# Two expert layers after a recurrent attention: the second one's weight conversion and loop order are changed

## The chip, the core and the metric

The kernel runs on one core of a Trainium2 chip. A core has a matrix engine (TensorE, PE in the rows, with PEld for its weight loads), a vector engine (VectorE, DVE), a scalar engine (ScalarE, ACT), a general engine (GpSimd, POOL) and SyncE (SP), which here issues all DMAs. Each engine works through its own queue in the order of the program and waits on semaphores of the others. SBUF is the on-chip memory of 128 partitions, PSUM the eight accumulator banks that PE writes. The metric is the device time of one execution in microseconds; lower is better.

## What is computed

A recurrent attention over 768 steps for 4 x 8 heads of width 40 gives a matrix x of 3072 tokens by 320. Two expert layers follow ("MoE 1" and "MoE 2"); no token is routed, all go through all weights:

```python
def _moe_ref(x, w_in, w_out):          # d_ff = 2048
    h = x @ w_in
    g = h * np.clip(h + 3.0, 0.0, 6.0) / 6.0
    return (g @ w_out).astype(np.float32)

def _moe2_ref(x, w_a, w_b, w_out):     # d_ff = 1536
    return ((x @ w_a) * (x @ w_b) @ w_out).astype(np.float32)
```

The expert weights come in as 64-bit floats. [...] Each float is then split into a rounded high part and a remainder, and a product is made of three matmuls (high x high, high x remainder, remainder x high).

## The kernel before

**Attention and MoE 1, side by side.** The attention is worked in chunks of 64 steps. `window(j)`, j = 0 to 11, lists the steps of chunk j (`op_a` to `op_g`, `prep_w`, `prep_kb`, ...). The table `MOE` sets behind which of them a step of MoE 1 stands (`up(i)` or `down(i)` of 256 tokens), and the word WEIGHT marks the places where a piece of weights is converted: seven in a window from j = 2 on. The list is the program's order on every engine. In window j, `t_store(j)` (L523) copies and sends off the triangular inverse that GpSimd has made (its ACT copy is L528); `op_a(j+1)`, `t_load(j+1)` and `t_start(j+1)` begin the next one: four stores to DRAM and a load that turn the layout (TA), then 62 GpSimd instructions in a row (L515, L518, the "solve"). Behind that, GpSimd has `prep_a(j+2)` (L453). `op_e` ends with two DVE instructions that write the mask product GH (L615), which `op_f`'s matmuls (L636) read. An `up` of MoE 1 is 16 matmuls of 256 columns, then on ACT a clipping (L313), on DVE the product (L314), on ACT the rounding (L129) and on DVE the remainder gl (L130); `down` is 12 matmuls of 320 columns and needs both parts.

**Conversion before.** `f32_steps` (L71) is one ACT instruction (L77) and five on DVE: L78 and L83 with one input, L80, L84 and L86 with two. `widen()` converts MoE 2's weights beside the attention: 68 pieces of 128 x 192. Each piece is loaded by SP, converted, and stored by SP as 32-bit floats to DRAM (`w2af`, `w2bf`, `w2of`). A window's seven WEIGHT places take seven pieces.

**MoE 1 after the attention.** Some 20 MoE 1 steps are left behind window 11. Between them stand `conv.go()` calls: they load the 32-bit floats and split them (ACT rounds, GpSimd and DVE by turns subtract), 16 of 36 pieces; the other 20 follow in the first group of MoE 2.

**MoE 2 before.** All weights lie split in SBUF. Outside runs g over six groups of 512 tokens, inside m over twelve blocks of 128 inner units. `up(g, m)` is 16 matmuls of 512 columns (two sums of eight, a and b), an ACT copy of a (L846), a DVE product (L848), and the split of it (L129, L130). `down(g, m-1)` follows, 12 matmuls of 320 columns into four accumulators, one for each 128 tokens; they collect all twelve m and are then copied out and stored (`store`). At m = 8 the next group's x is turned by PE (`trans`, L816 to L820).

Of the kernel before, what the change touches and what calls it, by code (L numbers as in the profile page):

```python
# [94 lines left out]
def attention_and_moe(ctx, tc, t, flag):  # L95
# [22 lines left out]
    w1 = m1.enter_context(tc.tile_pool(name="w1", bufs=1))  # L118
# [621 lines left out]
    WC = (("w2a", 3 * FF2), ("w2b", 3 * FF2), ("w2o", 12 * DM))  # L740
    w2f = {n: (dram.tile([128, c], F32, name=n + "f") if wide else t[n].rearrange("q k c -> q (k c)")) for n, c in WC}

    def widen():
        pieces = [(t[n].rearrange("q k c -> q (k c)")[:, c0:c0 + 192], w2f[n][:, c0:c0 + 192])
                  for n, cols in WC for c0 in range(0, cols if wide else 0, 192)]
        loaded, made = [], None
        for i in range(len(pieces) + 3):
            if made:
                sp.dma_start(out=made[0], in_=made[1])
                made = None  # L750
            if i < len(pieces):
                loaded.append((pieces[i][1], words(pieces[i][0], sp)))
            yield
            if loaded and (i > 1 or i >= len(pieces)):
                dst, st = loaded.pop(0)
                made = dst, from_words(st)
            yield

    def moe2_weights(pool):
        r = {}  # L760
        r["ah"] = pool.tile([128, 2, FF2], F32R, name="ah")
        r["al"] = pool.tile([128, 2, FF2], F32R, name="al")
        r["at"] = pool.tile([128, FF2], F32R, name="at")
        r["bh"] = pool.tile([128, 2, FF2], F32R, name="bh")
        r["bl"] = pool.tile([128, 2, FF2], F32R, name="bl")
        r["bt"] = pool.tile([128, FF2], F32R, name="bt")
        r["oh"] = pool.tile([128, 12, DM], F32R, name="oh")
        r["ol"] = pool.tile([128, 12, DM], F32R, name="ol")

        turn = [0]  # L770

        def load(src, n, sink, c0):
            st = wk1.tile([128, 384], F32, tag="ws", name="st", bufs=3)[:, 0:n]
            sp.dma_start(out=st, in_=src)

            def steps():
                turn[0] += 1
                yield sink(st, gp if turn[0] % 2 else ve)
            return n, steps()

        def up(nm, kt, cols):
            if kt < 2:
                return lambda st, eng: split(r[nm + "h"][:, kt, cols], r[nm + "l"][:, kt, cols], st, eng)
            return lambda st, eng: split_tail(r[nm + "t"][:, cols], st, eng)

        def dn(m):
            return lambda st, eng: split(r["oh"][:, m], r["ol"][:, m], st, eng)

        items = []
        for c in range(4):  # L790
            for kt in range(3):
                for nm in "ab":
                    c0 = kt * FF2 + 384 * c
                    items.append(((0, c), w2f["w2" + nm][:, c0:c0 + 384], 384, up(nm, kt, slice(384 * c, 384 * c + 384)), 0))
            items += [((1, m), w2f["w2o"][:, m * DM:m * DM + DM], DM, dn(m), 0) for m in range(3 * c, 3 * c + 3)]
        return r, Converter(items, load)

    def moe2(r, wk, xpool, conv):

        xs = {}  # L800

        def load_x(g):
            xin = xpool.tile([128, 4, 384], F32, tag="xin", name="xin")
            src = x2d[g * 512:(g + 1) * 512, :].rearrange("(n p) c -> p n c", p=128)
# [49 lines left out]
        def down(g, *ms):  # L854
# [14 lines left out]
            for m in ms:  # L869
                gs.pop((g, m))  # L870
# [348 lines left out]
```

## Time and profile before

| | us |
|---|---|
| median of 3 runs | 1393.04 (1391.51 to 1396.16) |
| profiled execution | 1393.52, span 1391.7 |
| busy: PE, DVE, POOL, ACT | 1144.8, 837.0, 526.3, 520.8 |
| start to 253 | windows 0 and 1, weights of MoE 1 converted |
| 253 to 933 | windows 2 to 11 |
| 933 to 977 | rest of MoE 1 |
| 977 to the end | MoE 2 |

Busy times are sums over stages with different limits; what binds in a stage has to be read from that stage. The profile dates each instruction, names what ended an engine's idle time in front of it ("<-"), and gives the granted clock of PE as a share of full speed (1.00 is 2.4 GHz, 0.50 is 1.2 GHz). A matmul's length in a row includes its way through the array; successive ones overlap, so a rate is read from start to start.

### The profile page before, as it was taken

To read this page: it belongs to the slowest core of one execution; us is meant where nothing else is said; L and a number is where in the kernel's file an instruction comes from. 1 tells how busy PE (TensorE), PEld (TensorE's weight loads), DVE (VectorE), ACT (ScalarE), POOL (GpSimd) and SP (SyncE) were. 2 spreads that over 40 slices of the span, in tenths; PEclk is the share of its full clock that TensorE was granted. 3 is DMA by queue.
4 is the path that set the end of the run, shared out by engine and by line. 5 is a ranking of instruction groups with operands and counts; after the bars stand their busy time and mean duration, and the time that the engine had idled before them with its cause. 6 is when DMAs were issued, how large, how long until landed. Compare 5 with 4: busy or idle time off the path is not lost.

```text
span 1391.7 us, 34838 instructions
## 1 busy us (share of the span) xinstructions
PE 1144.8 (82%) x14826; PEld 1039.0 (75%) x14826; DVE 837.0 (60%) x1297; ACT 520.8 (37%) x1071; POOL 526.3 (38%) x835
## 2 busy tenths in 40 slices
PE   1214439889798888888888889899999999999997
PEld 1214438878787787778878889799888888888886
DVE  7899777486867776777767776556532222222322
ACT  1243344445443444444344444345422222222221
POOL 4889008382818382747465656302200000000000
PEclk9998559989989899988898989899999999999999
DMA  6262451515142524242333333323410000000000
GB/s 175 50 161 68 108 137 30 138 53 141 58 115 68 130 72 119 74 125 76 106 96 107 95 92 80 97 74 105 128 28 20 24 19 23 20 23 20 2 18 22
DMA packets 139908, 107.82 MB, mean 77 GB/s; under 512 B 88448, under 2 KB 129024, under 8 KB 137728
## 3 DMA queue, kind: packets, MB, share of 16 engines
q1 hardware_dynamic: 139744, 105.51, 28.0%
q8 instruction: 118, 1.93, 0.6%
q14 instruction: 46, 0.38, 0.1%
HBM read 78.87 MB, written 26.61 MB: 76 GB/s over the span
## 4 chain that ended last, share of the span: by engine, by line
PE 39%; DVE 29%; DMA 11%; ACT 10%; issue 8%; SPq 2%; POOL 0%; DVEq 0%; ACTq 0%; POOLq 0%
PE att L842 19%; PE up L308 4%; PE ac L866 3%; PE ac L865 3%; PE ac L864 3%; DVE up L314 3%; DVE rw L448 3%; DVE cv L80 2%; DVE ws L84 2%; DMA n<-TA 2%; ACT sq L458 2%; ACT gh L129 2%; DVE ws L83 2%; DVE W L446 2%; ACT TA L528 2%
## 5 line engine op out<-in xcount | busy, mean ns | idle before, releaser
L515 POOL TENSOR_TENSOR TT<-TA,TN 64x31 f32<-64x31 f32 (+15 forms) x372 | 207.6, 558 | 323.9 <-DMA TA<-scr 295.5
L518 POOL TENSOR_TENSOR TN<-TN,TT 64x31 f32<-64x31 f32 (+15 forms) x372 | 220.1, 592 | 29.1
L848 DVE TENSOR_TENSOR g<-att,asb 128x512 f32<-128x512 f32 x72 | 49.8, 692 | 227.4 <-PE att L842 227.4
L328 PE MATMUL dn<-wo_h,gh 128*128 128x320 f32 x384 | 142.8, 372 | 14.7 <-ACT gh L129 14.6
L330 PE MATMUL dn<-wo_h,gl 128*128 128x320 f32 x384 | 135.1, 352 | 1.6 <-DVE gl L130 1.5
L329 PE MATMUL dn<-wo_l,gh 128*128 128x320 f32 x384 | 134.0, 349 | 0.0
L129 ACT CAST gh<-up 128x512 fp32r<-128x512 f32 x96 | 56.3, 586 | 185.4 <-DVE up L314 185.4
L308 PE MATMUL up<-xh,wi_h 128*128 128x256 f32 x384 | 108.2, 302 | 3.1 <-ACT xh L287 3.1
L130 DVE TENSOR_TENSOR gl<-up,gh 128x512 fp32r<-128x512 f32 x96 | 66.3, 691 | 62.6 <-ACT gh L129 62.6
L308 PE MATMUL up<-xh,wi_l 128*128 128x256 f32 x384 | 102.3, 288 | 0.0
L328 PEld LDWEIGHTS dn<-wo_h,gh 128*128 128x128 f32 x384 | 85.4, 222 | 20.6 <-ACT gh L129 16.1
L313 ACT ACTIVATE g<-up,bias 128x512 f32<-128x512 f32 x96 | 65.8, 686 | 91.8 <-PE up L308 90.7
L636 PE MATMUL att<-GH,KBT 128*64 128x64 f32 (+1 forms) x768 | 47.9, 285 | 62.0 <-DVE GH L615 60.7
L129 ACT CAST g2h<-g 128x512 fp32r<-128x512 f32 x72 | 44.7, 621 | 144.1 <-DVE g L848 144.1
L846 ACT COPY asb<-att 128x512 f32<-128x512 f32 x72 | 42.3, 587 | 147.6 <-PE att L842 147.6
L314 DVE SCALAR_TENSOR_TENSOR up<-g,up 128x512 f32<-128x512 f32 x96 | 66.0, 688 | 46.0 <-ACT g L313 46.0
L636 PEld LDWEIGHTS att<-GH,KBT 128*64 128x64 f32 (+1 forms) x768 | 39.7, 176 | 68.4 <-DVE GH L615 68.2
L864 PE MATMUL ac<-oh,g2h 128*128 128x320 f32 x288 | 88.8, 308 | 1.1 <-ACT g2h L129 1.1
L330 PEld LDWEIGHTS dn<-wo_h,gl 128*128 128x128 f32 x384 | 86.1, 224 | 4.6 <-DVE gl L130 4.6
L866 PE MATMUL ac<-oh,g2l 128*128 128x320 f32 x288 | 88.7, 308 | 0.2 <-DVE g2l L130 0.2
L865 PE MATMUL ac<-ol,g2h 128*128 128x320 f32 x288 | 88.8, 308 | 0.0
L448 DVE RECIPROCAL rw<-W 128x256 f32<-128x256 f32 x48 | 84.1, 1753 | 3.9 <-ACT sq L458 1.2
(170 smaller groups left out, 3050.8 us busy)
## 6 DMA issues: line engine op xcount, KB each, us to landing
RV<-in_rve_dram SPq DMA_DIRECT2D x24, 320.0 KB
KB<-in_kbe_dram SPq DMA_DIRECT2D x22, 320.0 KB
st<-in_w1i_dram SPq DMA_DIRECT2D x13, 384.0 KB
ws<-in_w2a_dram SPq DMA_DIRECT2D x24, 192.0 KB
ws<-in_w2b_dram SPq DMA_DIRECT2D x24, 192.0 KB
raw<-in_we_dram SPq DMA_DIRECT2D x24, 162.5 KB
LB<-in_ae_dram SPq DMA_DIRECT2D x24, 160.0 KB
VX<-in_vte_dram SPq DMA_DIRECT2D x24, 160.0 KB
```

The source lines that it names most:

```text
L129: ac.copy(out=hi, in_=src)
L308: mm(u[:, e], a_, b_, start=(n == 0), stop=(n == len(seq) - 1))
L328: mm(acc, gh[:, e, c0:c0 + 128], wo_h[:, m], start=(m == 0), stop=False)
L329: mm(acc, gh[:, e, c0:c0 + 128], wo_l[:, m], start=False, stop=False)
L330: mm(acc, gl[:, e, c0:c0 + 128], wo_h[:, m], start=False, stop=(m == 15))
L448: ve.reciprocal(out=rw, in_=w[:, :, 1:65])
L515: eng.tensor_tensor(out=tv, in0=TA[:, 0:u, u:u + 1].to_broadcast([nr, u, n]), in1=TN[:, u:u + 1, u:32].to_broadcast([nr, u, n]), op=ALU.mult)
L518: eng.tensor_tensor(out=TN[:, 0:u, u:32], in0=TN[:, 0:u, u:32], in1=tv, op=ALU.subtract)
L842: mm(u, a_, b_, start=(n == 0), stop=(n == len(seq) - 1))
L864: mm(acc, gh[:, sl], r["oh"][:, m], start=(m == 0), stop=False)
L865: mm(acc, gh[:, sl], r["ol"][:, m], start=False, stop=False)
L866: mm(acc, gl[:, sl], r["oh"][:, m], start=False, stop=(m == 11))
```

## The change

`widen()` and its 68 pieces are gone, and the windows' WEIGHT places stay empty once MoE 1's weights are converted. MoE 2 is turned round. Outside runs b over four blocks of three m (384 inner units), inside g over the six groups, then the three m. The four accumulators collect three m only; `total` then copies them to a sum on chip (b = 0; two by DVE, two by ACT) or adds them to it (b = 1 to 3; four DVE adds), 24 times four, and stores the sum after b = 3. All of x stays split in SBUF for the four passes. It is loaded and turned by 256 tokens (`trans(h)`), during the end of MoE 1 and the groups of block 0, one step behind another.

The weights come as words straight from the input: for each m two pieces of 256 columns for the rows 0 to 255 of a and b, one of 256 for the rest of both, and two of 160 columns for the output weights; 15 pieces a block, 60 in all. Each is loaded (two load buffers), converted by the same five DVE instructions and split, always with DVE. Block 0's 15 pieces stand in the end of MoE 1, a later block's in the steps of the block ahead of it, one a step. The product of a and b overwrites b's PSUM bank, which is then held until the remainder is made.

```diff
+        def ahead(self):
+            while self.todo and len(self.loaded) < 2:
...
+                    sp.dma_start(out=st[:, o:o + w].rearrange("q (k c) -> q k c", k=x.shape[1]), in_=x.bitcast(I32))
...
+        def go(self, last):
+
+            self.ahead()
+            if not self.loaded or self.loaded[0][0] > last:
+                return
+            m, i, st = self.loaded.pop(0)
+            if wide:
+                st = st.rearrange("q (c w) -> q c w", w=2)
+                cv = wk1.tile([128, 2, 256], I32, tag="cv", name="cv2", bufs=2)[:, :, 0:st.shape[1]]
+                w = to_f32(nc, st, cv[:, 0], cv[:, 1], st[:, :, 1])
...
+            if i < 2:
+                split(self.up[m][:, 4 * i:4 * i + 2], self.up[m][:, 4 * i + 2:4 * i + 4],
+                      w.rearrange("q (k c) -> q k c", k=2))
...
+            self.ahead()
...
-            ve.tensor_tensor(out=g_, in0=res[1], in1=asb, op=ALU.mult)
...
+            ve.tensor_tensor(out=res[1], in0=res[1], in1=asb, op=ALU.mult)
...
+        def total(g, b):
+            if b == 0:
+                sums[g] = (xr if g < 4 else left()).tile([128, 4, DM], F32, name=f"sum{g}")
+            for tt in range(4):
+                acc, o = accs[g][tt][:, 0:DM], sums[g][:, tt]
+                if b:
+                    ve.tensor_tensor(out=o, in0=acc, in1=o, op=ALU.add)
+                elif tt % 2:
+                    ac.copy(out=o, in_=acc)
+                else:
+                    ve.tensor_copy(out=o, in_=acc)
+                if (b + 1) * BLOCK == NM:
+                    r0 = 512 * g + 128 * tt
+                    sp.dma_start(out=t["out"][r0:r0 + 128, :], in_=o)
...
+            for b in range(NM // BLOCK):
+                for g in range(NG):
+                    for i in range(BLOCK):
+                        m = BLOCK * b + i
...
+                        up(g, m)
+                        if b == 0 and g + 1 < NG and i:
+                            trans(2 * g + 1 + i)
+                        if prev:
+                            down(*prev)
+                        prev = (g, m)
+                        if g or i:
+                            w2.go(BLOCK * b + 2 * BLOCK - 1)
...
         for j in range(NCH):
             for f in window(j):
...
-                    elif j:
-                        next(wide2, None)
-                        next(wide2, None)
...
             if n > WEIGHTS_2:
-                conv.go()
+                w2.go(BLOCK - 1)
             if n == RANGE:
                 decide()
+                load_x(0)
+        trans(0)
+        load_x(1)
         m1i.close()
-        wk2.append(c2.enter_context(tc.tile_pool(name="wk2", bufs=2, reuse_waits="tile")))
         mq.pop(0)()
-        trans_0()
+        trans(1)
         mq.pop(0)()
+        m1w.close()
```

Where instructions stand: DVE's queue in a window, from a store of Y to the second mask product GH. Before (cv and ws are buffers of one conversion each):

```order
L78 TENSOR_SCALAR ws<-cv_8146 128x192
L80 SCALAR_TENSOR_TENSOR cv_8146<-cv_8146,ws 128x192
L83 TENSOR_SCALAR ws<-cv_8146 128x192
L84 SCALAR_TENSOR_TENSOR ws<-ws 128x192
L86 TENSOR_TENSOR cv_8146<-cv_8146,ws 128x192
L615 TENSOR_TENSOR GH<-att,mask 128x512 x2
L78 TENSOR_SCALAR ws<-cv_8192 128x192
L80 SCALAR_TENSOR_TENSOR cv_8192<-cv_8192,ws 128x192
L83 TENSOR_SCALAR ws<-cv_8192 128x192
L84 SCALAR_TENSOR_TENSOR ws<-ws 128x192
L86 TENSOR_TENSOR cv_8192<-cv_8192,ws 128x192
L314 SCALAR_TENSOR_TENSOR up<-g,up 128x512
```

The same place in the changed kernel, DVE (its line numbers are one higher here):

```order
L638 TENSOR_TENSOR Y<-att,W_102 104x512
L616 TENSOR_TENSOR GH<-att,mask 128x512 x2
L315 SCALAR_TENSOR_TENSOR up<-g,up 128x512
L131 TENSOR_TENSOR gl<-up,gh 128x512
L638 TENSOR_TENSOR Y<-att,W_102 104x512
```

The ten conversion instructions around GH are gone; the rest stands as it stood.

DVE in the end of MoE 1, from xl (the remainder of the last 256 tokens) on. Before (bl is the remainder of a weight piece of b, x an output tile of MoE 1):

```order
L288 TENSOR_TENSOR xl<-xt,xh 128x768
L130 TENSOR_TENSOR bl<-st,bh 128x384
L334 TENSOR_SCALAR x_12158<-dn 128x320
L334 TENSOR_SCALAR x_12161<-dn 128x320
L314 SCALAR_TENSOR_TENSOR up<-g,up 128x512
L130 TENSOR_TENSOR gl<-up,gh 128x512
```

DVE at the same place in the changed kernel, from the third conversion to the fourth (up_11439 and dn_11528 are weight tiles of MoE 2, up without a number the PSUM bank of MoE 1):

```order
L78 TENSOR_SCALAR ws_11442<-cv_11486 128x256
L80 SCALAR_TENSOR_TENSOR cv_11486<-cv_11486,ws_11442 128x256
L83 TENSOR_SCALAR ws_11442<-cv_11486 128x256
L84 SCALAR_TENSOR_TENSOR ws_11442<-ws_11442 128x256
L86 TENSOR_TENSOR cv_11486<-cv_11486,ws_11442 128x256
L135 TENSOR_TENSOR up_11439<-cv_11486,up_11439 64x256
L315 SCALAR_TENSOR_TENSOR up<-g,up 128x512
L131 TENSOR_TENSOR gl<-up,gh 128x512
L78 TENSOR_SCALAR ws_11466<-cv_11521 128x160
L80 SCALAR_TENSOR_TENSOR cv_11521<-cv_11521,ws_11466 128x160
```

Where one subtraction stood between two products of MoE 1, there are now one or two whole conversions of six DVE instructions.

DVE in the first group of MoE 2 before (g and g2l are a product and its remainder, ol and al remainders of weights):

```order
L848 TENSOR_TENSOR g_12720<-att,asb 128x512
L130 TENSOR_TENSOR g2l<-g_12720,g2h 128x512
L130 TENSOR_TENSOR al<-st,ah 128x384
L848 TENSOR_TENSOR g_12770<-att,asb 128x512
L130 TENSOR_TENSOR g2l<-g_12770,g2h 128x512
```

DVE in one step of block 0 of the changed kernel (x2l is the remainder of the next group's x):

```order
L852 TENSOR_TENSOR att<-att,asb 128x512
L131 TENSOR_TENSOR g2l<-att,g2h 128x512
L832 TENSOR_TENSOR x2l_12409<-att,x2h_12408 128x3x128 x2
L78 TENSOR_SCALAR ws_12377<-cv_12498 128x256
L80 SCALAR_TENSOR_TENSOR cv_12498<-cv_12498,ws_12377 128x256
L83 TENSOR_SCALAR ws_12377<-cv_12498 128x256
L84 SCALAR_TENSOR_TENSOR ws_12377<-ws_12377 128x256
L86 TENSOR_TENSOR cv_12498<-cv_12498,ws_12377 128x256
L135 TENSOR_TENSOR up_12374<-cv_12498,up_12374 64x256
```

A whole conversion and the next group's x now stand behind the product of every step of block 0.

## Rows read from the trace of the kernel before

**Rows 1.** Stretches: length, busy us (xinstructions) PE PEld DVE ACT POOL; clock, DMA share, GB/s.

```profile
542.83:614.57 71.74, 60.34 (x1059) 56.00 (x1059) 52.65 (x80) 31.62 (x69) 40.84 (x66) 0.88 0.38 104
...
828.08:888.27 60.19, 55.38 (x1052) 52.52 (x1044) 39.01 (x68) 28.62 (x59) 33.59 (x62) 0.94 0.35 89
...
933.00:977.00 44.00, 43.08 (x324) 42.05 (x323) 26.05 (x39) 22.82 (x44) 9.31 (x9) 1.00 0.38 117
977.00:1391.70 414.70, 405.20 (x2083) 350.15 (x2081) 124.09 (x191) 107.38 (x196) 9.95 (x9) 0.99 0.09 28
```

**Rows 2.** Chain of waits, 200 to 960: start us, length us, link (two L528).

```profile
253.17 1.95 ACT TA L528
...
828.08 1.96 ACT TA L528
```

**Rows 3.** DVE by line, 200 to 900: xcount | busy us, mean ns | idle before.

```profile
L80 DVE SCALAR_TENSOR_TENSOR cv<-cv,ws 128x192 int32<-128x192 int32 x66 | 46.1, 698 | 2.3
L84 DVE SCALAR_TENSOR_TENSOR ws<-ws 128x192 f32<-128x192 uint32 (+1 forms) x67 | 42.7, 638 | 2.3
L86 DVE TENSOR_TENSOR cv<-cv,ws 128x192 f32<-128x192 f32 (+1 forms) x67 | 38.5, 575 | 2.3
...
L83 DVE TENSOR_SCALAR ws<-cv 128x192 int32<-128x192 int32 x66 | 30.4, 461 | 2.3
...
L78 DVE TENSOR_SCALAR ws<-cv 128x192 int32<-128x192 int32 x66 | 25.9, 392 | 5.3 <-ACT cv L77 5.3
```

**Rows 4.** Waits, 200 to 900: who for whom, total us, times, longest us.

```profile
PE att L636 <- DVE GH L615: 48.3, 27, 4.7
...
ACT cv L77 <- DMA w2bf<-cv: 25.8, 8, 6.5
```

**Rows 5.** PE in order of time, window 10: start us, length us, line [idle before].

```profile
875.49 2.53 PE L636 MATMUL att<-GH,KBT 128*64 128x64 f32 x32 [4.68 <-DVE GH L615]
...
879.18 0.47 PE L329 MATMUL dn<-wo_l,gh 128*128 128x320 f32 x1
```

**Rows 6.** GpSimd (POOL) in order of time, windows 6 and 10.

```profile
562.34 0.25 POOL L515 TENSOR_TENSOR TT<-TA,TN 64x31 f32<-64x31 f32 x1 [29.09 <-DMA TA<-scr]
...
602.06 4.96 POOL L453 TENSOR_TENSOR LB<-LB,W 64x1024 f32<-64x1024 f32 x2
...
845.45 0.25 POOL L515 TENSOR_TENSOR TT<-TA,TN 64x31 f32<-64x31 f32 x1 [23.21 <-DMA TA<-scr]
...
883.57 0.25 POOL L518 TENSOR_TENSOR TN<-TN,TT 64x31 f32<-64x31 f32 x1
```

**Rows 7.** DVE in order of time, one conversion while GpSimd is idle.

```profile
903.70 0.25 DVE L78 TENSOR_SCALAR ws<-cv 128x192 int32<-128x192 int32 x1
...
905.07 0.36 DVE L86 TENSOR_TENSOR cv<-cv,ws 128x192 f32<-128x192 f32 x1
```

**Rows 8.** DVE in order of time, MoE 1 after the attention.

```profile
944.50 0.96 DVE L288 TENSOR_TENSOR xl<-xt,xh 128x768 fp32r<-128x768 f32 x1
...
973.95 0.70 DVE L314 SCALAR_TENSOR_TENSOR up<-g,up 128x512 f32<-128x512 f32 x1 [0.46 <-ACT g L313]
975.30 0.69 DVE L130 TENSOR_TENSOR gl<-up,gh 128x512 fp32r<-128x512 f32 x1 [0.65 <-ACT gh L129]
```

**Rows 9.** DVE in order of time, two steps of MoE 2.

```profile
996.63 0.69 DVE L848 TENSOR_TENSOR g<-att,asb 128x512 f32<-128x512 f32 x1 [1.75 <-PE att L842]
998.01 0.69 DVE L130 TENSOR_TENSOR g2l<-g,g2h 128x512 fp32r<-128x512 f32 x1 [0.69 <-ACT g2h L129]
...
1002.13 0.69 DVE L848 TENSOR_TENSOR g<-att,asb 128x512 f32<-128x512 f32 x1 [2.28 <-PE att L842]
```

**Rows 10.** DVE and then ScalarE in order of time: the two halves of a split.

```profile
983.89 0.48 DVE L130 TENSOR_TENSOR ol<-st,oh 128x320 fp32r<-128x320 f32 x1
...
983.16 0.46 ACT L129 CAST oh<-st 128x320 fp32r<-128x320 f32 x1
```

**Rows 11.** PE in order of time, the last step of MoE 2.

```profile
1380.53 0.41 PE L864 MATMUL ac<-oh,g2h 128*128 128x320 f32 x1 [1.06 <-ACT g2h L129]
```

More of the change, by code (lines that the diff above doesn't have):

```diff
@@ L736, in window @@
         return out
[L740 to L796, printed above, removed]
@@ L805, in load_x, with moe2, trans @@
+    def moe2(w2, xr, left):
+        xins, xs, gs, accs = {}, {}, {}, {}
+        sums = {}
+        def load_x(h):
+            xin = wk1.tile([128, 2, 384], F32, tag=("xt", "xh", "xl")[(h - 1) % 3 if h > 1 else 0], name="xin", bufs=1)
+            src = x2d[h * 256:(h + 1) * 256, :].rearrange("(n p) c -> p n c", p=128)
             sp.dma_start(out=xin[:, :, 0:DM], in_=src)
             sp.dma_start(out=xin[:, :, DM:384], in_=src[:, :, 256:DM])
-            xs[g] = xin
-        def trans(g):
-            xin = xs.pop(g)
-            xh = wk().tile([128, 3, 512], F32R, tag="x2h", name="x2h")
-            xl = wk().tile([128, 3, 512], F32R, tag="x2l", name="x2l")
-            for n in range(4):
+            xins[h] = xin
+        def trans(h):
+            xin = xins.pop(h)
+            g, c = h // 2, 256 * (h % 2)
+            if h % 2 == 0:
+                pool = xr if g < 2 else left()
+                xs[g] = [pool.tile([128, 3, 512], F32R, name=f"x2{n}{g}") for n in "hl"]
+            xh, xl = xs[g]
+            for n in range(2):
@@ L817, in trans @@
                 pv = ps[:, 0:384].rearrange("q (k c) -> q k c", k=3)
-                ac.copy(out=xh[:, :, 128 * n:128 * n + 128], in_=pv)
-                ve.tensor_tensor(out=xl[:, :, 128 * n:128 * n + 128], in0=pv,
-                                 in1=xh[:, :, 128 * n:128 * n + 128].bitcast(F32), op=ALU.subtract)
-            xs[g] = (xh, xl)
-        NG = NT // 512
-        accs = {}
-        gs = {}
+                cols = slice(c + 128 * n, c + 128 * n + 128)
+                ac.copy(out=xh[:, :, cols], in_=pv)
+                ve.tensor_tensor(out=xl[:, :, cols], in0=pv, in1=xh[:, :, cols].bitcast(F32), op=ALU.subtract)
         def up(g, m):
-            conv.need(0, m // 3)
+            w2.need(m, False)
             xh, xl = xs[g]
-            f0 = 128 * m
+            w = w2.up[m]
             res = []
-            for nm in "ab":
+            for i in range(2):
                 u = bank()
@@ L881, in rest @@
         def rest():
-            load_x(1)
             prev = None
-            for g in range(NG):
-                for m in range(12):
-                    up(g, m)
-                    if g == 0:
-                        conv.go(3)
-                    if prev and (g, m) != (NG - 1, 11):
-                        down(*prev)
-                        prev = None
-                    prev = prev + (m,) if prev else (g, m)
-                    if m == 8 and g + 1 < NG:
-                        trans(g + 1)
-                        if g + 2 < NG:
-                            load_x(g + 2)
+            load_x(2)
@@ new lines, in rest @@
+            for b in range(NM // BLOCK):
+                for g in range(NG):
+                    for i in range(BLOCK):
+                        m = BLOCK * b + i
+                        if b == 0 and g + 1 < NG:
+                            h = 2 * g + 2 + i
+                            if i < 2:
+                                load_x(h + 1) if h + 1 < 2 * NG else None
+                        up(g, m)
[6 more added lines that the diff above has]
+                            w2.go(BLOCK * b + 2 * BLOCK - 1)
```

116 lines of the change are left out of this document (68 added, 48 removed).

## Prediction

> **What bounds the kernel now.** I read the stretches first, cut where window j of the attention begins its store (L528, t_store) [rows 1]. Two regimes show. From 977 us to the end (MoE 2) PE is busy 405.2 of 414.7 us at clock 0.99, while DVE works 124 us of it: PE bounds that stage, DVE is 70% idle. In the windows nothing is full: in window 6 PE is busy 60.3 of 71.7 us at granted clock 0.88, DVE 52.7, POOL 40.8. The chain of waits gives the length: L528 of window 2 at 253.17, of window 10 at 828.08 [rows 2], so eight windows of 71.9 us each. At full clock PE's work in a window is about 60.3 x 0.88 = 53 us (in window 10: 55.4 x 0.94 = 52 us). So some 19 us of a window are PE idle or at the lower clock.
>
> Then what holds PE there. The groups by line show the five DVE instructions of a conversion (L78 to L86): together 183.6 us of DVE between 200 and 900, 2.76 us for each of some 67 pieces, 19.3 us for the seven pieces of a window [rows 3]. They stand in DVE's queue between the MoE's products and the masks GH, and PE waits for GH 48.3 us in all; ACT stands besides, 25.8 us in one of several such rows, because a conversion buffer has not yet been written out [rows 4]. What such a wait costs shows in window 10: PE idles 4.68 us before L636, which then takes 2.53 us, and the matmuls of 320 columns after it have 0.47 us each [rows 5]; those are the rates of the lower clock level (1.2 of 2.4 GHz), granted after the idle time.
>
> Is there another limit just below 71.9? POOL's triangular solve is the candidate. In window 6 its data lands at 562.34, 19.5 us after L528, and it ends at 602.06, 39.7 us later; the next L528 comes at 614.57, 12.5 us after that. In window 10 it starts 17.4 us after L528 and takes 38.4 us [rows 1, 6].
>
> **Part 1, the windows.** The 68 pieces leave windows 2 to 11, with their ACT instruction and both DMAs; nothing else there is reordered (the first two fences of the change show DVE's queue at GH). DVE keeps 52.7 - 19.3 = 33.4 us of work per window. The floor from PE is 53 us. The floor from POOL is 19.5 + 39.7 = 59.2 us at window 6's prices, 17.4 + 38.4 = 55.8 us at window 10's, since L528 copies what the solve has made. Window 10 is a trial of the whole: it lacks the preparation of later windows, so DVE has 39.0 us there with the pieces still in, and it takes 60.2 us [rows 1]. The other windows would have a lighter DVE than that. I take 59.2, the POOL chain at the prices of the window itself, and keep 55.8 to 64.2 as bounds (64.2 is a rival below). Gain: 8 x (71.9 - 59.2) = 101.3 us. Window 10 falls from 60.2 to its POOL chain of 55.8: 4.4 us. Window 11 has no solve beside it and PE nearly full: nothing. Together 105.7 us. The matching SP work goes too, but SP only releases loads there; I cost it at nothing, covered by the POOL chain, which contains SP's transfers and is kept at today's 19.5.
>
> **Part 2, the end of MoE 1.** The first 15 pieces now stand between the last eight ups of MoE 1, two to most ups (the fourth fence). POOL does nothing beside them. A piece of 192 columns with POOL idle takes 1.73 us from 903.70 to 905.43 [rows 7]: 0.25 us with one input, 0.36 with two. With 0.48 us for 320 columns [rows 10] a column costs 0.94 ns, so 256 columns take 2 x 0.31 + 3 x 0.42 + gaps 0.15 = 2.03 us and 160 take 1.58. Then ACT rounds (0.46 at 320 columns [rows 10], so 0.40 and 0.31) with DVE waiting, and DVE subtracts (0.42 and 0.33); three hand-overs of 0.05. A piece holds DVE 3.0 us (nine of 256) or 2.4 us (six of 160): 41.4 us for 15. Each up needs 0.70 + 0.65 wait + 0.69 = 2.04 us of DVE [rows 8], and 0.3 more because ACT's clipping now stands behind a rounding: 2.34 x 8 = 18.7 us. With 0.9 us for two stores that is 61.0 us from the end of xl (945.46). Today the same stretch ends with gl at 975.99, 30.5 us after xl [rows 8]: PE sets the pace there, and the splits beside it hide. So DVE becomes the bound and the stage grows by 30.5 us; 1 us more for PE's lower clock when it starts again: **+31.5**. Bounds: +20 if the rounding hides behind the next piece, +46 if a piece costs what it costs beside POOL (2.76 x 256/192 = 3.7, with the split 4.5).
>
> **Part 3, MoE 2 itself.** The matmuls are the same, 16 of 512 and 12 of 320 columns a step, and a step is 5.50 us on PE (996.63 to 1002.13) [rows 9]. DVE has 2.07 us in it (product, wait for ACT, remainder [rows 9]). In block 0 three steps (the last fence) also have two copies of sums (0.96), four remainders of x (1.95, at the price of rows 10), three pieces (8.3) and about 0.6 us behind ACT's rounding: 18.0 us, against 16.5 us of PE plus its transposes (at most 18.7/5 = 3.7 per group, what 72 x 5.50 leaves of the stage's 414.7 [rows 1]). Further, the second half of x for the next group is made one step before it is used, not three: PE waits some 0.6 us five times. Block 0: +4 us. In blocks 1 and 2 the four adds of 0.48 replace copies and transposes: 17.0 us against 16.5, half a microsecond late per group, and PE asks for a remainder only a whole step after its product, so 3.4 us of slack covers it; block 3 has no pieces. If the cover were gone it would cost 2.5 us a block. The four accumulators must be emptied before the next group's first down; an up of 3.7 us stands between, and four adds are 1.9 us. At the end today PE waits 1.06 us for the last product [rows 11] and restarts at the lower clock; now a whole down stands before it: -1.5. Sum of part 3: **+2.5**. Bounds: -2 and +40 (the rival of DVE).
>
> **Sum** against the profiled execution (1393.52 us, span 1391.7; the median of the runs, 1393.04, is the same within their spread): 1393.5 - 105.7 + 31.5 + 2.5 = **1322 us**.
>
> **One rule against the rows.** In window 6 the two-input conversion instructions take 0.58 to 0.70 us on average [rows 3] and 0.36 with POOL idle [rows 7]: so far it is DVE that waits when both work. If part of that waiting falls on POOL instead, each of the five pieces that lie in a solve holds POOL for 3 x 0.36 = 1.1 us, the solve would shrink from 39.7 to 34.3, and the window to 53.8 us, near PE's 53: 1393.5 - 8 x 18.1 - 5 + 34 = 1278 us. The Trainium skill, SBUF — State Buffer, Who interferes with whom, says this of the pair: a VectorE instruction with two SBUF inputs and a GpSimd one that reads SBUF exclude one another, and whichever comes second blocks fully. Against it stands window 10's solve, still 38.4 us with five pieces beside it but fewer other DVE instructions [rows 6].
>
> **Rivals.** (a) *POOL's loop is longer than I count.* Behind the solve POOL prepares an input of the window after next (prep_a, L453, 4.96 us [rows 6]), and the next solve's input needs them. If nothing overlaps it, a window is 19.5 + 39.7 + 5.0 = 64.2 us: gain 8 x 7.7 + 4.4 = 66, time 1362. For it: all three are one queue. Against: the store's transfers run during L453. (b) *DVE bounds MoE 2.* If pieces cost 3.7 us on average there, three steps need 20 to 21 us in block 0 and 20 in blocks 1 and 2 against 16.5 to 17.7: +40 us instead of +2.5, time 1360. Against: POOL is idle then, and rows 7 shows what that does. (c) *Denser windows*, 55.8 us as in window 10's chain: gain 8 x 16.1 + 4.4 = 133, time 1294. (d) *Slower.* The windows keep their length, because SP's and POOL's chain through L528 is refilled by another wait (key loads, say) as soon as DVE is free; then only the 34 us of parts 2 and 3 remain: 1427. It decides from a window of 67.7 us on (34 / 8 = 4.2 us saved). Against: POOL is idle for 12.5 us before L528 in window 6, and window 10 took 60.2 with its pieces. (e) The rule above: 1278.
>
> **How the numbers follow.** Forecast 0.60, (a) 0.14, (b) 0.09, (c) 0.10, (e) 0.03, (d) 0.03, and 0.01 for a gain that just cancels. The range leaves out (e), (d) and half of the edges: 1288 to 1368. Faster by over 0.3% (about what a measurement here can tell from no change) 0.95, within it 0.02, slower 0.03.
>
> **What would show it.** Right: L528 at intervals near 59 us; no wait of PE on GH; POOL's end close before L528; DVE full and PE at the lower clock for some 60 us after the attention; steps of 5.5 us in MoE 2, a little more in block 0. Wrong: L528 intervals above 64, or DVE full in blocks 1 and 2 with PE waiting for remainders or accumulators.

## The result: 1317.4 us, and the profile after

The changed kernel takes 1317.38 us (median of 4 runs, 1316.93 to 1321.99), the kernel before in the same comparison 1392.28 us (1386.87 to 1396.16): a ratio of 0.947, 95% interval 0.943 to 0.951. The forecast was 1322 us, with a range of 1288 to 1368. The profiled execution spans 1315.7 us against 1391.7. Cut at the same places, the two spans differ as follows (L529 is the former L528; line numbers up to L738 are one higher now):

| stretch, us | before | after | difference | forecast |
|---|---|---|---|---|
| start to L529 of window 2 | 253.2 | 251.3 | -1.9 | 0 |
| windows 2 to 9 | 574.9 | 478.3 | -96.6 | -101.3 |
| window 10 | 60.2 | 57.4 | -2.8 | -4.4 |
| window 11 to the end of xl | 57.2 | 53.6 | -3.6 | 0 |
| end of xl to end of the last gl | 30.5 | 58.2 | +27.7 | +31.5 |
| from there to the end (MoE 2) | 415.7 | 416.9 | +1.2 | +2.5 |
| sum | 1391.7 | 1315.7 | -76.0 | -71.7 |

The start is between 245 and 257 us in the runs below, so its 1.9 us show nothing.

The stretches of the changed kernel, with the columns of [rows 1]: window 6, window 10, the end of MoE 1 and what follows it up to MoE 2's first up, and a hundred microseconds from the middle of MoE 2.

```profile
490.53:548.97 58.44, 55.20 (x1072) 52.20 (x1072) 33.62 (x45) 29.48 (x62) 38.74 (x66) 0.97 0.33 85
...
729.62:787.02 57.40, 54.47 (x1068) 51.73 (x1069) 21.82 (x33) 26.50 (x51) 36.89 (x66) 0.97 0.26 63
...
840.60:898.79 58.19, 39.66 (x226) 36.45 (x224) 42.34 (x112) 19.96 (x47) 0.00 (x0) 0.82 0.25 76
898.79:904.17 5.38, 4.54 (x19) 4.55 (x20) 2.54 (x6) 1.00 (x3) 0.00 (x0) 0.50 0.07 19
...
1003.00:1101.00 98.00, 98.00 (x505) 85.38 (x504) 62.73 (x146) 30.41 (x68) 0.00 (x0) 1.00 0.12 35
```

Window 6 against [rows 1]: DVE works 33.6 us instead of 52.7 (forecast 33.4), PE 55.2 instead of 60.3, at 0.97 instead of 0.88 of the full clock. In the end of MoE 1 PE stands at 0.82, with DVE at work for 42.3 of 58.2 us. In MoE 2 PE is full.

The ACT copy that opens a store, in order of time; it answers [rows 2]: (729.62 - 251.32) / 8 = 59.8 us a window, where before had 71.9 and the forecast 59.2.

```profile
251.32 1.92 ACT L529 COPY TA<-TN 32x1024 f32<-32x1024 f32 x1
...
548.97 1.92 ACT L529 COPY TA<-TN 32x1024 f32<-32x1024 f32 x1
...
729.62 1.94 ACT L529 COPY TA<-TN 32x1024 f32<-32x1024 f32 x1
```

GpSimd in window 6, answering [rows 6]: the solve's first and last instruction, and prep_a behind it.

```profile
509.41 0.25 POOL L516 TENSOR_TENSOR TT<-TA,TN 64x31 f32<-64x31 f32 x1 [14.71 <-DMA TA<-scr]
...
548.65 0.25 POOL L519 TENSOR_TENSOR TN<-TN,TT 64x31 f32<-64x31 f32 x1
548.97 4.38 POOL L454 TENSOR_TENSOR LB<-LB,W 64x1024 f32<-64x1024 f32 x2
```

The solve ends at 548.90 and L529 starts at 548.97: no more 12.5 us between them. What lies between one solve and the next is in the chain of waits (start us, us, what), from prep_a behind the solve of the window before:

```profile
489.20 2.16 POOL LB L454
...
491.44 2.17 POOL LB L454
493.65 1.16 PE att L482 x62
494.81 3.17 PE up L309 x16
...
500.60 0.58 ACT AB L485
...
502.43 2.12 DMA scr<-AB
504.67 4.61 DMA TA<-scr
```

So the loop is solve (39.5), prep_a (4.4), the op_a that reads it (L482), an up and its product that stand behind it in the queues, ACT's copy AB, the stores and the load of scr: GpSimd's round, as forecast, but by way of prep_a. PE's waits between 490 and 730 are one row where [rows 4] had GH first, and that row is nearly all of PE's idle time there (15.0 us in four windows):

```profile
PE att L482 <- POOL LB L454: 14.9, 8, 2.6
```

The end of MoE 1, DVE in order of time: the first piece, from L78 to the next piece's L78 2.81 us, and the end of the last gl, where [rows 8] had 975.99.

```profile
840.52 0.29 DVE L78 TENSOR_SCALAR ws<-cv 128x256 int32<-128x256 int32 x1
...
842.09 0.43 DVE L86 TENSOR_TENSOR cv<-cv,ws 128x256 f32<-128x256 f32 x1
842.99 0.42 DVE L131 TENSOR_TENSOR up<-cv,up 128x256 fp32r<-128x256 f32 x1 [0.47 <-ACT up L130]
843.33 0.29 DVE L78 TENSOR_SCALAR ws<-cv 128x256 int32<-128x256 int32 x1
...
898.10 0.69 DVE L131 TENSOR_TENSOR gl<-up,gh 128x512 fp32r<-128x512 f32 x1 [0.65 <-ACT gh L130]
```

Who waits there (840 to 899; total us, times, longest), on PE and on ACT:

```profile
PE dn L329 <- ACT gh L130: 16.1, 6, 6.3
ACT up L130 <- DVE cv L86: 13.7, 6, 2.6
ACT dn L130 <- DVE cv L86: 11.7, 6, 2.0
ACT up L134 <- DVE cv L86: 6.5, 3, 2.3
```

PE waits 16 us for products, and ACT stands 31.9 us with a rounding at the head of its queue that waits for a conversion's last DVE instruction. One wait there had not been forecast: PE, in order of time, before the second `trans`, for tokens that are still being loaded; MoE 2's first up follows behind a down at the lower clock, 5.4 us after the last gl.

```profile
899.62 1.54 PE L828 MATMUL att<-ident,xin 128*128 128x128 f32 x6 [2.65 <-DMA xin<-x2d]
...
904.17 0.63 PE L847 MATMUL att<-x2h,up 128*128 128x512 f32 x1
```

In MoE 2 the only idle time of PE before its ups is 2.0 us, in the page's groups:

```profile
L847 PE MATMUL att<-x2l,up 128*128 128x512 f32 x432 | 170.7, 395 | 2.0 <-DVE x2l L832 2.0
```

### The profile page after: what moved, and what is told of

The parts are those of the page before. It is cut to its first block, busy times and chain, and to the rows that moved or that the text cites. A ratio compares the mean times of both kernels' runs of the same rounds, so it can differ in the third digit from the quotient of the medians.

```text
span 1315.7 us, 34806 instructions
## 1 busy us (share of the span) xinstructions
PE 1106.6 (84%) x14826; PEld 1010.3 (77%) x14826; DVE 793.0 (60%) x1371; ACT 516.7 (39%) x1087; POOL 502.1 (38%) x817
## 4 chain that ended last, share of the span: by engine, by line
PE 45%; POOL 24%; DVE 12%; DMA 7%; issue 6%; ACT 4%; SPq 1%; POOLq 0%; DVEq 0%; ACTq 0%
PE att L847 20%; POOL TN L519 11%; POOL TT L516 10%; PE up L309 6%; PE ac L871 3%; PE ac L870 3%; PE ac L869 3%; POOL LB L454 3%; DMA TA<-scr 2%; PE att L482 1%; PE dn L329 1%; DMA scr<-AB 1%; PE dn L331 1%; PE dn L330 1%; DVE cv_p L78 1%
## 5 line engine op out<-in xcount | busy, mean ns | idle before, releaser
L847 PE MATMUL att<-x2h,up 128*128 128x512 f32 x720 | 237.4, 394 | 0.0
L847 PE MATMUL att<-x2l,up 128*128 128x512 f32 x432 | 170.7, 395 | 2.0 <-DVE x2l L832 2.0
L847 PEld LDWEIGHTS att<-x2h,up 128*128 128x128 f32 x720 | 135.4, 188 | 29.0
L329 PE MATMUL dn<-wo_h,gh 128*128 128x320 f32 x384 | 129.4, 337 | 17.4 <-ACT gh L130 17.4
L852 DVE TENSOR_TENSOR att<-att,asb 128x512 f32<-128x512 f32 x72 | 50.4, 700 | 98.0 <-PE att L847 80.8
L130 ACT CAST gh<-up 128x512 fp32r<-128x512 f32 x96 | 56.2, 586 | 102.7 <-DVE up L315 102.7
L847 PEld LDWEIGHTS att<-x2l,up 128*128 128x128 f32 x432 | 81.2, 188 | 19.4 <-DVE x2l L832 3.5
L482 PE MATMUL att<-LB,KB 40*64 40x64 f32 x1408 | 40.8, 275 | 63.9 <-POOL LB L454 30.9
L869 PE MATMUL ac<-dn,g2h 128*128 128x320 f32 x288 | 89.5, 311 | 0.0
L482 PEld LDWEIGHTS att<-LB,KB 40*64 40x64 f32 x1408 | 35.4, 185 | 70.4 <-POOL LB L454 34.4
L871 PE MATMUL ac<-dn,g2l 128*128 128x320 f32 x288 | 88.6, 308 | 0.1
L870 PE MATMUL ac<-dn,g2h 128*128 128x320 f32 x288 | 88.7, 308 | 0.0
```

The lines of the kernel that those rows point to most:

```text
L329: mm(acc, gh[:, e, c0:c0 + 128], wo_h[:, m], start=(m == 0), stop=False)
L482: mm(pss[ab][half(c), i], KB[rows(ab), p, 64 * c:64 * c + 64], lb[rows(ab), ab, p], start=True, stop=True)
L847: mm(u, a_, b_, start=(n == 0), stop=(n == len(seq) - 1))
L869: mm(acc, gh[:, sl], w[:, 0], start=(i == 0), stop=False)
L870: mm(acc, gh[:, sl], w[:, 1], start=False, stop=False)
L871: mm(acc, gl[:, sl], w[:, 0], start=False, stop=(i == BLOCK - 1))
```

## The experiments

All runs in one table. "window" is the mean of windows 2 to 9 by L529 (L528 in kernels made from before), "end" the time from the end of xl to the end of the last gl, both of the profiled execution; the ratio is to the kernel before, with its 95% interval.

| run | window | end | median us | ratio |
|---|---|---|---|---|
| before | 71.9 | 30.5 | 1392.3 | 1 |
| the changed kernel | 59.8 | 58.2 | 1317.4 | 0.947 (0.943 to 0.951) |
| e1_none | 59.8 | 30.5 | 1289.0 | 0.925 (0.918 to 0.931) |
| e1b_moves | 60.2 | 30.5 | 1294.4 | 0.929 (0.922 to 0.935) |
| e8_no_stores | 70.5 | 30.5 | 1384.6 | 0.997 (0.994 to 1.000) |
| e3_pieces_back | 70.8 | 58.0 | 1417.5 | 1.019 (1.012 to 1.026) |
| e4_prep_a_on_dve | 58.8 | 58.0 | 1303.1 | 0.937 (0.930 to 0.944) |
| e5_block0_away | 64.7 | 30.5 | 1321.1 | 0.948 (0.943 to 0.954) |
| e5b_block0_at_GH | 63.2 | 30.5 | 1313.8 | 0.945 (0.941 to 0.950) |
| e6_both | 64.1 | 30.5 | 1313.9 | 0.945 (0.941 to 0.950) |
| e7_squares_in_g | 64.1 | 30.5 | 1320.6 | 0.951 (0.943 to 0.958) |
| e2_block0_unconverted | 59.6 | 31.0 | 1286.8 | 0.923 (0.917 to 0.930) |
| e9_tail_gp | 59.1 | 59.9 | 1307.2 | 0.940 (0.934 to 0.945) |
| e10_late_rounding | 59.0 | 51.4 | 1300.5 | 0.933 (0.929 to 0.937) |

### What of the pieces cost the windows their 12 us

A piece is converted from 64-bit floats, read as pairs of 32-bit words, to 32-bit floats. **e1_none**: the pieces gone, MoE 2 as before, but on stand-in weights.

```diff
     def widen():
-        pieces = [(t[n].rearrange("q k c -> q (k c)")[:, c0:c0 + 192], w2f[n][:, c0:c0 + 192])
...
+        sp.dma_start(out=w2f.rearrange("q (k c) -> q k c", k=3), in_=ident[:, None, :].to_broadcast([128, 3, 128]))
+        yield
```

> The kernel before, without the 68 pieces beside the attention: no load, no conversion, no store; MoE 2 reads the same 196 kB of stand-in weights for every piece. All else, MoE 2's order too, is before's. Theory (the windows fall to GpSimd's loop, and all of the forecast's gain lies there): windows of 59.8 us as in the changed kernel and the stretch up to xl shorter by the 105 us that the two traces show, so 1392.3 - 105 = 1287 us, below the changed kernel by its longer end of MoE 1. Rival (the turned MoE 2 gives a part of the gain): above 1317.

1289.0 us: as the theory has it. Without the pieces, and with nothing else changed, 103 us go, and the turned MoE 2 is no part of the gain.

**e1b_moves**: loads and stores stay, the conversion goes.

```diff
-                made = dst, from_words(st)
+                made = dst, wo_h[:, 0, 0:192].bitcast(F32)
```

> The kernel before with the 68 loads and 68 stores left as they are, but no conversion between them: the stores send a constant piece of another tile. So SyncE's queue and the DMA traffic are before's, while DVE and ACT are free of the pieces. Theory (DVE's time was the price of the pieces, SyncE's is covered by GpSimd's loop): within 6 us of the run without any piece, about 1287 to 1293, windows of 60 to 60.5 us. Rival (the pieces' DMAs in SyncE's queue hold the stores and loads of the loop through L528): a good part of the length stays, windows of 66 us and more, 1335 us or above. Between them each has its share, to be read from the windows.

1294.4 us, 5.4 more than without any piece; a window is 60.2 us. One of its windows (columns of [rows 1]), with 0.44 of the DMA engines' time in use instead of 0.33 and the same length:

```profile
490.51:549.33 58.82, 55.46 (x1072) 52.31 (x1072) 34.05 (x45) 29.48 (x62) 39.31 (x67) 0.97 0.44 119
```

SyncE's work and the traffic were thus worth half a microsecond a window, which the forecast had put at nothing. Window 11 up to the end of xl is 58.2 us here and 53.7 in e1_none (57.2 before): the 3.6 us that the changed kernel gained there, also forecast at nothing, go with the loads and stores.

**e8_no_stores**: the other half, conversion without stores. ACT's waits for a buffer that is still to be sent off, in [rows 4], were the other candidate.

```diff
             if loaded and (i > 1 or i >= len(pieces)):
-                dst, st = loaded.pop(0)
-                made = dst, from_words(st)
+                from_words(loaded.pop(0))
```

> The kernel before with the 68 pieces loaded and converted, but never stored; MoE 2 reads 196 kB of stand-in weights. DVE has all its 19 us of conversion in a window, ACT its part; only the stores are gone, and with them every wait of ACT for a conversion buffer to be sent off (L77 two times in a window for about 6 us, the squares L458 for 3.5 us). Theory of DVE (the forecast's: the pieces' time in DVE's queue is what they cost): windows of 69 us and more, 1365 us or above. Theory of the buffer (ACT, stopped by a store that stands in SyncE's queue behind stores and loads waiting for something else, is late with what the loop needs): windows of 63 us and less, 1320 us or below. Between: each has its share, as the window shows.

1384.6 us, windows of 70.5: the conversion itself is the price (its ACT and its five DVE instructions together; no run separates them), and those waits of ACT cost at most 1.4 us of a window. A window of it, and then PE's wait for GH between 538 and 821:

```profile
538.90:612.08 73.18, 61.26 (x1074) 56.81 (x1073) 52.80 (x80) 31.50 (x69) 41.13 (x66) 0.88 0.37 97
```

```profile
PE att L636 <- DVE GH L615: 23.9, 13, 4.5
```

PE's work is the same as in the changed kernel: 61.26 x 0.88 = 53.9 us at full clock against 55.20 x 0.97 = 53.5. The 14.7 us more of this window, a long one set against a short one, are 8.7 us of idle time and 6.1 us of the same work at a lower clock. On average over windows 2 to 9 the kernel before has 10.4 us of PE's idle time and 61.4 us of its work, the changed kernel 3.6 and 56.2: of the 12.1 us, 6.9 are idle time and 5.2 PE's work at a lower clock.

**e3_pieces_back**: the changed kernel, with before's `widen()` and its two calls at each WEIGHT place again.

```diff
+                    elif j:
+                        next(wide2, None)
+                        next(wide2, None)
```

> The changed kernel, with the 68 pieces put back beside the attention, loads, conversions and stores, seven a window as before; what they store is not read. Theory (the windows' gain and the end of MoE 1's loss are separate and add): windows of 72 us again and 1317.4 + 105 = 1422 us, about the 1427 us of the forecast's slower rival. Rival (the pieces cost that much only together with something else that the change removed): windows of 66 us or less, below 1375 us.

1417.5 us (1412.9 and 1422.1): the two parts of the change add. It is also close to the time that the forecast's slower rival would have had, had the windows kept their length.

### Which loop sets the windows

**e4_prep_a_on_dve**

```diff
-            + on(nx2, (prep_a, j + 2, gp), (prep_sq, j + 2)))
+            + on(nx2, (prep_a, j + 2), (prep_sq, j + 2)))
```

> The changed kernel with one instruction pair moved: the preparation of an input of the window after next (prep_a, L454, 4.4 us on GpSimd behind the solve) is done by DVE instead, at the same place in the program. Theory A (it is a link of GpSimd's loop: solve, prep_a, op_a, up, ACT's AB, the stores of scr, TA, solve): windows shorter by 1 to 4 us each, 1317.4 - 8 x (1 to 4) = 1285 to 1309 us. Theory B (the loop goes from the end of the solve through L529 and the store's DMAs on SyncE, as the forecast had it, and prep_a lies beside them): windows change by under 1 us, 1310 to 1322 us. Slower than that if DVE's 4 to 5 us stand in front of masks that PE waits for.

1303.1 us. The windows fall by 1.0 us, at the low edge of theory A and under what prep_a's 4.4 us would give; five of the 17.4 us between the two spans come before window 2 (one to three in the two later runs that keep only this edit beside the attention). From the end of a solve to the start of the next it is 17.5 us on average in windows 2 to 9 instead of 20.1: prep_a was in the loop. More than half of this came back in the solve, on average 41.0 us instead of 39.4. GpSimd beside DVE's L454 (each in order of time):

```profile
597.69 1.25 POOL L519 TENSOR_TENSOR TN<-TN,TT 64x87 f32<-64x87 f32 x1
599.01 1.15 POOL L516 TENSOR_TENSOR TT<-TA,TN 64x60 f32<-64x60 f32 x1
```

```profile
597.52 2.50 DVE L454 TENSOR_TENSOR LB<-LB,W 64x1024 f32<-64x1024 f32 x2
```

Two instructions of 0.35 and 0.28 us take 1.25 and 1.15 while DVE's pair runs: 1.8 us in this solve. PE, no longer stopped by LB, now waits for MoE 1's products instead, 8.6 us between 484 and 718.

The solve still closes a window: L529 starts within 0.25 us of its end in seven of the eight, as in this row of ACT.

```profile
601.20 2.07 ACT L529 COPY TA<-TN 32x1024 f32<-32x1024 f32 x1 [0.75 <-POOL TN L519]
```

But the chain of waits that leads to that solve's start no longer meets prep_a. It goes back through PE's queue, without a break from 511 to 552, to a store two windows earlier:

```profile
484.22 2.02 ACT TA L529
...
511.14 0.64 PE dn L329
...
560.22 0.26 POOL TT L516
```

So the solve and PE's queue lie in one loop here, 117 us for two windows (484.22 to 601.20). A bound that does without the solve is not shown by this run.

### Are a few pieces hidden beside the attention?

By the forecast's floors (PE 53, GpSimd 59) three pieces a window should cost nothing, and block 0's weights could leave the end of MoE 1. **e5_block0_away** and **e5b_block0_at_GH** differ in the places alone; the pieces are stored as floats in `w20` and read from there. The first edit is e5_block0_away's; the other run has (3, 4, 6).

```diff
+                    elif j and slot in (1, 2, 7):
+                        next(wide2, None)
+                        next(wide2, None)
...
-            if wide:
+            if wide and m >= BLOCK:
                 st = st.rearrange("q (c w) -> q c w", w=2)
```

> The changed kernel, with block 0's weights alone converted beside the attention again: 24 pieces of 128 or 160 columns, three a window, at the first, second and last of the seven places, none of them between the masks GH and the matmuls that read them; stored as floats, and only loaded and split in the end of MoE 1. Theory (GpSimd's loop sets the window and hides three such pieces, 3 x 2 us of DVE; the end of MoE 1 falls to 31 us): windows within 0.7 us of 59.8, time 1317.4 - 30 = 1287 us (1284 to 1293). Rival (a piece costs a window its share whatever the loop does): 3/7 x 12.1 us x 136/192 = 3.7 us a window, 8 x 3.7 = 29 us, so nothing is gained: about 1316 us.

> As the run before it in this list, the same 24 pieces, three a window, but at the third, fourth and sixth of the seven places: just behind an op_e and ahead of the op_f that reads its GH. Theory of number (only DVE's amount counts, and the loop hides it): the same time, 1284 to 1293 us. Theory of place (a piece ahead of GH makes PE idle for its 2 us, and the waits push the work that ends in the next store): windows 2 us and more above those of the run before, 1303 us or above; and PE's waits for GH, none in the changed kernel, are back.

1321.1 and 1313.8 us. The end of MoE 1 fell to 30.5 us, 27.7 less, and the windows took it all back: 64.7 and 63.2 us. Of the 24 pieces 22 lie in these eight windows, so each cost 1.8 and 1.2 us. My theory was wrong; the rival, a price by the piece, is near. The theory of place finds no support, since ahead of GH was not dearer, but the pair does not decide it: PE waits for GH in both, 11.0 us in four windows of e5_block0_away and 9.6 in four of e5b_block0_at_GH. A window of e5_block0_away, and PE's largest wait between 507 and 769:

```profile
507.54:572.81 65.27, 59.19 (x1126) 55.38 (x1118) 39.71 (x60) 30.35 (x65) 40.87 (x66) 0.92 0.32 86
```

```profile
PE att L637 <- DVE GH L616: 11.0, 6, 2.9
```

Against the changed kernel's window 6 it has 6.8 us more: 2.8 of PE's idle time and 4.0 of PE's work at 0.92 instead of 0.97 of the clock (on average 4.9 us: 2.8 and 2.1). GpSimd is not what binds: its solve ended at 566.74, and L529 came at 572.81.

What binds shows in the chain of waits. In e5b_block0_at_GH it goes from one L529 to the next, 63.9 us later, and does not meet the solve: ACT's copies AB, DVE's LB, the load of KB and DVE's work on it, GH, two of the pieces, the second GH, PE's L637 and an up, and then ACT's queue, where L529 stands last.

```profile
567.07 2.01 ACT TA L529
...
607.37 1.05 DVE GH L616 x2
608.48 0.55 DVE ws L78
...
618.78 1.41 PE att L637 x30
...
630.97 1.95 ACT TA L529
```

The two pieces hold DVE for 3.5 and 3.0 us beside the solve; one of 128 columns takes 1.4 us where GpSimd is idle (e5_block0_away, 522.55). Without them this loop would be some 57 us, an estimate from this window (63.9 - 3.5 - 3.0), so it lies only a little under GpSimd's 59.8.

**e7_squares_in_g** tests whether it is not DVE's time but a buffer. Just ahead of that L529 ACT's squares had waited for a piece's store:

```profile
570.85 1.06 ACT L459 ACTIVATE sq<-W 128x1024 bf16<-128x1024 f32 x1 [0.44 <-DMA w<-cv]
...
572.81 2.08 ACT L529 COPY TA<-TN 32x1024 f32<-32x1024 f32 x1
```

```diff
-        tag, bufs = ("g", 1) if room["wide"] else ("cv", 2)
+        tag, bufs = "g", 1
```

> The run with block 0's pieces at the first, second and last place, and one word changed: ACT's squares (L458 there) write their unused result into the buffer g of MoE 1's clipping, not into one of the two conversion buffers, so they no longer wait for a piece's store. Theory of the buffer: the 1.75 us of a window that ACT waited there, and what stood behind it (RH, then L529), come back: windows of 60 to 62 us, time 1287 to 1300 us. Theory of DVE (3 pieces of 1.6 us cost that much in any case): windows of 64 us and 1315 to 1321 us as without the change.

1320.6 us, windows of 64.1: the buffer is worth at most 0.6 us of a window.

**e6_both** is e5_block0_away with e4's edit.

> Block 0's pieces at the first, second and last place and prep_a on DVE together. If the two gains are of separate stages they add: 1317.4 - 14.3 - 30 = 1273 us (1269 to 1280). If DVE's 2.5 us for prep_a and its 6 us for the pieces meet in one window and the loop, shorter by a microsecond or two, hides less of them: 1280 to 1290 us.

1313.9 us: worse than both theories, since each had block 0's pieces hidden; windows of 64.1 us, as without prep_a on DVE. With pieces in the windows GpSimd's loop is not the bound, so a shorter one gives little there.

### What holds the end of MoE 1

**e2_block0_unconverted**

```diff
+            if wide and m < BLOCK:
+                w = st.rearrange("q (c w) -> q c w", w=2)[:, :, 1].bitcast(F32)
+            elif wide:
```

> The changed kernel, but block 0's 15 pieces of MoE 2's weights are loaded and split without the conversion (the high words stand in for the floats); 15 ACT and 75 DVE instructions go from the end of MoE 1. Theory (DVE bounds that stage because of the pieces): 15 pieces lose 9 x 2.0 + 6 x 1.6 = 27.6 us of DVE; the stage then falls back nearly to what PE sets, xl to the last gl 31 to 36 us instead of 58.2, and the time to 1317.4 - 25 = 1292 us (1289 to 1297). Rival (the rounding on ACT and the split hold the stage as much as the conversion): 40 us and more from xl to gl, 1300 us or above.

1286.8 us, 30.6 less, with 31.0 us from xl to gl and PE full again:

```profile
842.27:873.29 31.02, 29.76 (x226) 29.00 (x224) 17.21 (x36) 15.09 (x31) 0.00 (x0) 1.00 0.45 139
```

The 15 conversions are the whole loss of that stage. Behind it 2.8 us more go (873.29 to 1287.4 is 414.1, where the changed kernel takes 416.9): 2.0 of them between the last gl and the first up, where PE now runs at the full clock, 3.4 us instead of 5.4.

**e9_tail_gp** (with e4's edit, so 1303.1 us is its reference) gives the remainders to GpSimd.

```diff
-                split_tail(self.up[m][:, 8:10], w.rearrange("q (k c) -> q k c", k=2))
+                split_tail(self.up[m][:, 8:10], w.rearrange("q (k c) -> q k c", k=2), gp if m < BLOCK else ve)
```

> The changed kernel with prep_a on DVE, as in the run that measured 1303.1 us, and block 0's 15 remainders (L131, L135) on GpSimd, which is idle in the end of MoE 1, instead of DVE. Theory (DVE bounds the stage with 3.0 and 2.4 us a piece; it loses the subtraction of 0.42 or 0.33 us and the wait of about 0.45 for ACT's rounding): 15 x 0.8 = 12 us, xl to the last gl 46 us instead of 58, time 1291 us (1288 to 1295). Rival (GpSimd beside DVE makes the two-input conversion instructions longer, as it did beside the attention, by up to 0.7 us a piece): no gain or 2 to 3 us, 1300 us and above.

1307.2 us, 59.9 us from xl to gl: no gain, but not for the rival's reason either. The two-input conversion instructions are as short as without GpSimd (0.43 and 0.33 us). Only L78, with one input, is longer in six of the 15 pieces (0.40 to 0.70 us instead of 0.29 or 0.24), 1.8 us in all. DVE in order of time, then ACT:

```profile
843.59 0.33 DVE L86 TENSOR_TENSOR cv<-cv,ws 128x160 f32<-128x160 f32 x1
844.90 0.69 DVE L315 SCALAR_TENSOR_TENSOR up<-g,up 128x512 f32<-128x512 f32 x1 [0.98 <-ACT g L314]
```

```profile
843.95 0.33 ACT L130 CAST dn<-cv 128x160 fp32r<-128x160 f32 x1 [2.09 <-DVE cv L86]
844.18 0.68 ACT L314 ACTIVATE g<-up,bias 128x512 f32<-128x512 f32 x1
```

ACT holds the rounding at the head of its queue until DVE's L86 is done, 2.09 us; the clipping, whose input is there, stands behind it, and DVE then waits for the clipping. In the changed kernel DVE's subtraction ran beside that clipping and was free.

**e10_late_rounding** moves rounding and remainder one piece later and changes nothing else of e9.

```diff
+                steps = f32_steps(nc, st, cv[:, 0], cv[:, 1], st[:, :, 1])
+                steps[0]()
+                self.flush()
+                for step in steps[1:]:
+                    step()
...
+            self.late.append((m, lambda: self.parts(m, i, w)))
```

> As the run with prep_a on DVE and block 0's remainders on GpSimd (1307.2 us), with one thing changed in the order: a piece's rounding on ACT (L130, L134) and its remainder stand one piece later, behind the next piece's first ACT instruction (L77), in MoE 2 as well. So ACT's clipping of MoE 1 and the next L77 no longer stand behind a rounding that waits for DVE's last instruction of the same piece. Theory (in the end of MoE 1 DVE and ACT wait for one another by turns, and the 58 to 60 us are DVE's 8 x 1.39 for the ups, 28 for the conversions, and the waits): xl to the last gl falls to 44 to 49 us, time 1307 - 13 = 1294 us (1289 to 1298). Rival (the stage is held elsewhere, by the loads of the pieces or by PE): 55 us and more, 1302 us or above.

1300.5 us, 6.7 less than e9, and 51.4 us from xl to gl: the theory's cause, but only 8.5 of the 11 to 16 us it asked for. The remaining part shows in DVE, now beside GpSimd's remainders (DVE, then GpSimd, in order of time):

```profile
832.14 0.76 DVE L83 TENSOR_SCALAR ws<-cv 128x256 int32<-128x256 int32 x1
...
836.33 0.95 DVE L80 SCALAR_TENSOR_TENSOR cv<-cv,ws 128x256 int32<-128x256 int32 x1
```

```profile
832.01 0.74 POOL L131 TENSOR_TENSOR up<-cv,up 128x256 fp32r<-128x256 f32 x1 [55.53 <-ACT up L130]
836.27 0.73 POOL L131 TENSOR_TENSOR up<-cv,up 128x256 fp32r<-128x256 f32 x1 [3.52 <-ACT up L130]
```

0.29 became 0.76 and 0.43 became 0.95. L83 is longer in five of the 15 pieces and L80 in seven; with L78 that is 5.1 us. This run has the lowest median of those that compute everything, and its interval lies below that of the changed kernel, but from e4's, without the two later edits, it cannot be told apart.

## Why the prediction was right, and where it was not

**Part 1, the windows: right in size, by a way that is partly another.** The chain through L529 at 59.2 us measured 59.8, DVE's 33.4 us 33.6, and PE's wait for GH went as foretold. Window 10 took 57.4, not 55.8. But the forecast priced the way from L528 over the store to the solve, 19.5 us; what bound is prep_a and the op_a behind it, 20.1 us from one solve to the next. That the two are so nearly alike is luck. Rival (a) had this mechanism, prep_a in the loop, but no length of its own: it runs beside the store's transfers, as its counterargument said, and 64.2 us did not come.

PE's floor of 53 us was not put to the test by the change, since PE's idle time in these windows is its wait for prep_a. As a measure of what else fits into a window it failed: that GpSimd's chain hides three pieces, on which I built e5, was an error of 34 us. DVE, ACT and PE hand work to each other in a loop that is only a little shorter than GpSimd's, and the forecast had no such loop.

12.1 us for seven pieces are 1.73 us for each, and 1.73 us is what a conversion takes alone [rows 7]; nothing shows that this is more than a coincidence. A piece takes 2.76 us in the windows [rows 3], and the price was not the same everywhere: window 2 of the two e5 runs, with one piece, took 61.4 and 60.9 us (59.6 to 61.5 in the changed kernel, e1_none and e2), and window 10, with two, 54.6 us (57.4 without).

**Part 2, the end of MoE 1: +31.5 forecast, +27.7 measured.** A piece of 256 columns took 2.81 us instead of 3.0, one of 160 some 2.3 instead of 2.4: 9 x 0.19 + 6 x 0.1 = 2.3 us less. The 1 us for PE's lower clock came too, but behind the last gl, in the next row of the table. "DVE becomes the bound" was half right: the conversions set the stage (e2), but DVE works only 42.3 of its 58.2 us. The rest is two engines waiting for each other in their queues' order (e9, e10). The forecast had those waits in its sum, and counted them as time in which a piece or an up holds DVE.

**Part 3, MoE 2: +2.5 forecast, +1.2 measured**, of two signs. From the last gl to the first up it is 5.4 us instead of 1.8 (before: 975.99 to 977.79): the wait for tokens, which no step had, and the lower clock. From the first up to the end it is 411.5 instead of 413.9, 2.4 us less: the middle of the stage has PE full, and its waits for remainders in block 0 are 2.0 us in all, where I had +4 for that block. The cover of 3.4 us held. Rival (b) did not come.

**Rivals (c), (d), (e).** Windows of 55.8 us (c) did not come, not even with prep_a off GpSimd (e4, 58.8). (d) is near e3_pieces_back's time, not this kernel's. (e): the solve would have shrunk from 39.7 to 34.3 us; it measured 39.5 without the pieces. In the windows it was DVE that had waited, 0.58 to 0.70 us for what takes 0.36 alone [rows 3, 7].

**The sum.** The rows of the first table miss their forecasts by -3.8 to +4.7 us; the misses are of both signs and leave 4.3 us of 71.7. The total is nearer than its parts.

**Open.** The loop of DVE, ACT and PE is read from chains of waits, and its 57 us without pieces are an estimate; no run isolates it. Nor is it shown whether three pieces ahead of GH would cost more than three that keep clear of it, since neither of the two runs kept PE from waiting for GH. Fewer than three pieces a window had no run of their own. The later rounding was not tried without e4's edit and GpSimd's remainders.

## What to carry over

An engine's work at full clock is not its floor: engines that hand work to and fro in their queues' order make a loop, and the loops have to be compared before anything is called hidden. Here one lay a little under the other, and three pieces put into it cost 3.4 to 4.9 us a window. Work in a queue that feeds a nearly full PE was paid for in two ways here: of the 12.1 us of seven pieces 6.9 were idle time and 5.2 a lower clock. In a stage where two in-order engines hand work to and fro, put the instruction that must wait behind those that are ready: taking work off the busier engine gave nothing here, that reordering 6.7 us.

## What the runs showed of the hardware

GpSimd and DVE stop each other in both directions. Two GpSimd instructions of 0.35 and 0.28 us took 1.25 and 1.15 beside a DVE pair of 1.24 us each with two inputs (e4); DVE's L80 took 0.95 instead of 0.43 beside a GpSimd subtraction (e10). The Trainium skill, SBUF — State Buffer, Who interferes with whom, says that a DVE instruction with two SBUF inputs and a GpSimd one that reads SBUF exclude each other and that issue order decides who blocks; these rows agree. What it would have made of this change, rival (e), did not come: in the windows the short conversion instructions waited for the solve, and taking them away left the solve as long as it was. That sentence is on two inputs; L83, which has one, took 0.76 instead of 0.29 us beside a GpSimd subtraction (e10).
